# The inverse transform's second stage in 64x64 tiles, in a gated mix of two state-space convolutions

## The chip, the cores and the metric

The kernel runs on one core of a Trainium2 chip. The core has TensorE (PE in the profile; its weight loads are listed apart as PEld), VectorE (DVE), ScalarE (ACT), GpSimd (POOL) and SyncE (SP, which issues every DMA here). The metric is the time of one execution in microseconds on the device; less is better. Before the change it is 507.52 us, the median of three runs (505.0 to 507.69). All data are float32.

## The reference

Two state-space models with their own parameters filter the same signal `u` (2048 steps, 512 channels), and a gate mixes the results. For each channel d, the 128 states n are summed into a kernel K of 2048 taps, and u is convolved with it by FFT. Cut to what matters:

```
g = sigmoid((u * gate_w).sum(-1))                  # one number per time step
# model A (model B is alike, with exp(log_A_real), 2.0 and no B)
K = einsum("dn,dnl,dn->dl", C, exp(dt * A * l), dt * B).real
a = irfft(rfft(u, 2L) * rfft(K, 2L))[:L] + u * Dskip
return g * a + (1 - g) * b
```

## The kernel before, in words

**Tiles.** The 512 channels are cut into eight tiles v of 64 channels, taken in pairs q = v // 2 (four pairs of 128 channels). Each tile holds both models, k = 0 and 1. A time step is l = 64 j + s, with 32 values of j and 64 of s, so a transform of 2048 points is one over j (32 points, the "first stage") and one over s (64 points, 32 different matrices for the indices m, the "second stage").

**A tile's way.** For each of eight chunks of 16 channels (`chunk`) the states' powers are made as tables: POOL multiplies phases and magnitudes (L552, L561, L572, L580: two times 512 elements of `x`, then 512 and 1024 of `E`), ACT takes sine, absolute value and cosine (L592 to L594, 1024 elements each, into the PSUM buffers `sd`), DVE multiplies (L600 to L615), and PE sums over the 128 states (L631, tiles of 128x32) into the bank `kg`. After every second chunk ACT copies the bank to `K` (L653), and `put` does the first stage: 32 matmuls of 64x64 tiles (L674) into two PSUM banks, each copied to `F` by DVE or ACT, as the masks `EV` and `EU` say (L686). When `F` is full, `stage2` takes the 32 indices m in eight groups mg of four: `forward` (L697: four matmuls of 128x128 by 128 columns with `c_g`), the product with the spectrum of u in two DVE operations (L769 and L772: 512 elements each, with the real and the sign-turned imaginary part of u, into `z`), the inverse (L781 and L782: eight matmuls of 128x128 by 128 columns with `c_t`, in pairs that accumulate), a copy by ACT (L785) and a store to HBM (`wt`, L788).

**u.** For each pair, `stage1_u` and `stage2_u` do the same forward transform on u; its spectrum goes to HBM (`ud`, L739) and comes back per tile (L760), 512 KB for two groups mg.

**The end of a pair.** `final` loads `wt` back in another layout (L803) and does the inverse's other stage with weights that contain the gate (L814, 128x64 tiles), in four banks. The loads and sums of a pair come after both its tiles. For the last pair the four loads of a tile go to the buffers in `LAST`.

**The gate.** `gate` sums u * gate_w on PE with a broadcast weight (L843), copies (L852), takes the sigmoid on ACT (L854, 2048 elements), and POOL multiplies it into the weights (L861, L873: 16 operations each of 128x4x32).

**The order.** `Plan` collects operations, each with an engine, a cost, a due time, the buffers that it takes and the operations that it needs. `Plan.run` plays a clock and gives each engine the ready operation that is due first and has its buffers free, and the kernel then issues all of them in that order. So each engine works through a fixed list, and waits where an operand or a buffer is late. The numbers in the tables at the top (`TO`, `LAG`, `FSP` and so on) are due times. SP's list of DMAs is fixed in the same way, and eight semaphores go round: a DMA is issued only once the eighth one before it has landed.

**PSUM.** Eight banks of 128x512: four single ones (`ps`: one for `kg`, two for `forward`, two for `put`, all four for the rest, within the caps), and two double ones (`sd`, 1024 elements) for sine and cosine alone.

## Time and profile before

| What | us |
|---|---|
| median of three runs (505.0 to 507.69) | 507.52 |
| the profiled execution | 506.61 |
| its span, from the first to the last instruction | 504.8 |
| PE busy | 422.9 |
| DVE busy | 398.2 |
| POOL busy | 393.8 |
| ACT busy | 388.8 |

The granted clock of TensorE was 0.949 on average. In the profile's rows, a group of instructions stands as line, engine, operation, out<-in, shape and count, then total busy time in us and mean ns of one, then the engine's idle time before such instructions and who ended it. A row of the timeline is start in us, duration in us, and then the same names. A float32 matmul leaves two records, so counts of matmul records are twice those of the matmuls in the code. A busy time is a union: where instructions of an engine overlap at their ends, that time counts once.

### The profile page before, as it was taken

How to read it: one execution, taken by the hardware profiler on the slowest of the kernel's cores; microseconds unless marked ns; L12 is line 12 of the kernel's file. 1: busy time of each engine (PE TensorE's matmuls, PEld its weight loads, DVE VectorE, ACT ScalarE, POOL GpSimd, SP SyncE). 2: the span in 40 equal slices, each digit the busy share in tenths (PEclk: the TensorE clock that was granted, in tenths of full speed). 3: DMA queues.
4: the chain of work that ended last, by engine and by line, in shares of the span. 5: the costliest groups of instructions: out<-in, count | busy, mean ns of one | idle time of the engine just before them, and what ended most of it. 6: DMA issues, size and time to landing. Idle time of an engine off the chain costs nothing.

```text
span 504.8 us, 21830 instructions
## 1 busy us (share of the span) xinstructions
PE 422.9 (84%) x9584; PEld 383.2 (76%) x9584; DVE 398.2 (79%) x564; ACT 388.8 (77%) x598; POOL 393.8 (78%) x365
## 2 busy tenths in 40 slices
PE   3497996788989999998289986598999899799946
PEld 3397895777767898888279875488989799789936
DVE  5748998989939889999859988978979999863420
ACT  4659989789999887799998778857999878562111
POOL 4674997979969999989898999768979999920000
PEclk9999997699999999999669999789999999989988
DMA  8958773254654455444208676347336157753954
GB/s 284 382 159 270 225 222 122 86 181 117 153 171 130 138 185 149 127 128 128 62 7 248 197 236 214 107 139 219 106 114 195 34 157 229 218 156 115 307 164 189
DMA packets 69438, 85.45 MB, mean 169 GB/s; under 512 B 4704, under 2 KB 50144, under 8 KB 69088
## 3 DMA queue, kind: packets, MB, share of 16 engines
q1 hardware_dynamic: 69344, 84.06, 53.5%
q8 instruction: 75, 1.23, 1.0%
q14 instruction: 19, 0.16, 0.1%
HBM read 50.49 MB, written 33.59 MB: 167 GB/s over the span
## 4 chain that ended last, share of the span: by engine, by line
PE 45%; ACT 20%; DMA 15%; DVE 8%; issue 7%; POOL 3%; SPq 1%; DVEq 0%; ACTq 0%; POOLq 0%
PE ps L697 10%; PE ps L631 8%; PE ps L781 7%; PE ps L782 7%; PE ps L674 6%; PE ps L814 5%; DMA wt<-st 4%; DMA c_g<-in_c_g 3%; DMA X<-wt 3%; ACT sd L592 3%; ACT sd L594 2%; ACT x L593 2%; DMA AB<-in_prm 2%; ACT st L785 2%; DVE z L772 2%
## 5 line engine op out<-in xcount | busy, mean ns | idle before, releaser
L580 POOL TENSOR_TENSOR E<-AB 128x1024 f32<-128x1024 f32 x64 | 125.4, 1960 | 0.1
L781 PE MATMUL ps<-z,c_t 128*128 128x128 f32 x512 | 102.6, 282 | 3.7 <-DVE z L772 1.6
L782 PE MATMUL ps<-z,c_t 128*128 128x128 f32 x512 | 99.9, 277 | 1.2 <-DVE z L772 0.8
L600 DVE TENSOR_TENSOR QD<-sd,E 128x1024 f32<-128x1024 f32 x64 | 77.8, 1216 | 20.3 <-ACT sd L592 9.4
L631 PE MATMUL ps<-E 128*32 128x64 f32 x2048 | 68.1, 230 | 24.5 <-DVE E L610 17.5
L697 PE MATMUL ps<-F,c_g 128*128 128x128 f32 x640 | 85.7, 281 | 3.5 <-ACT F L686 1.3
L781 PEld LDWEIGHTS ps<-z,c_t 128*128 128x128 f32 x512 | 77.6, 191 | 9.0 <-DVE z L772 3.3
L697 PEld LDWEIGHTS ps<-F,c_g 128*128 128x128 f32 x640 | 77.4, 191 | 8.0 <-ACT F L686 1.6
L782 PEld LDWEIGHTS ps<-z,c_t 128*128 128x128 f32 x512 | 77.7, 192 | 2.8 <-DVE z L772 2.7
L631 PEld LDWEIGHTS ps<-E 128*32 128x32 f32 x2048 | 50.9, 115 | 36.5 <-issue 18.9
L561 POOL TENSOR_TENSOR x<-pi,c_tm 128x512 int32<-128x512 int32 x64 | 68.0, 1064 | 13.1 <-ACT sd L594 12.0
L610 DVE TENSOR_TENSOR E<-sd,E 128x1024 f32<-128x1024 f32 x64 | 77.6, 1213 | 0.8 <-ACT sd L594 0.8
L572 POOL TENSOR_TENSOR E<-AB 128x512 f32<-128x512 f32 x64 | 68.5, 1072 | 8.7 <-issue 2.8
L592 ACT ACTIVATE sd<-x 128x1024 f32<-128x1024 int32 x64 | 65.9, 1030 | 9.0 <-DVE QD L605 7.6
L785 ACT COPY st<-ps 128x512 f32<-128x512 f32 x64 | 37.5, 586 | 44.3 <-PE ps L782 25.1
L552 POOL TENSOR_TENSOR x<-gh 128x512 int32<-128x512 int32 x64 | 68.7, 1074 | 0.2
L593 ACT ACTIVATE x<-x 128x1024 f32<-128x1024 int32 x64 | 67.8, 1060 | 1.3
L594 ACT ACTIVATE sd<-x 128x1024 f32<-128x1024 f32 x64 | 66.0, 1032 | 2.6 <-DVE E L615 0.9
L631 PE MATMUL ps<-QD 128*32 128x64 f32 x2048 | 67.1, 228 | 0.1
L769 DVE TENSOR_TENSOR z<-ps,U 128x512 f32<-128x512 f32 x64 | 43.8, 684 | 27.1 <-PE ps L697 23.7
L631 PEld LDWEIGHTS ps<-QD 128*32 128x32 f32 x2048 | 53.0, 116 | 0.0
L674 PE MATMUL ps<-w,K 64*64 64x64 f32 x2048 | 41.0, 230 | 9.0 <-DVE fi L454 3.4
(118 smaller groups left out, 748.9 us busy)
## 6 DMA issues: line engine op xcount, KB each, us to landing
U<-ud SPq DMA_DIRECT2D x32, 512.0 KB, 4.1
wt<-st SPq DMA_DIRECT2D x64, 256.0 KB, 2.7
X<-wt SPq DMA_DIRECT2D x26, 512.0 KB, 5.6
ud<-z SPq DMA_DIRECT2D x32, 256.0 KB, 3.4
U<-in_u SPq DMA_DIRECT2D x16, 256.0 KB, 4.2
ud<-z SPq DMA_DIRECT2D x32, 128.0 KB, 3.4
U<-in_uT SPq DMA_DIRECT2D x16, 256.0 KB, 3.4
out<-st SPq DMA_DIRECT2D x16, 256.0 KB, 5.7
```

Source lines behind the costliest of these rows:

```text
L552: G.tensor_tensor(xi()[:, :, 1, :].rearrange("n c (a b) -> n c a b", a=4), t[:, :, 0:4].unsqueeze(3).to_broadcast([P, NCK, 4, 8]), t[:, :, ...
L580: G.tensor_tensor(Ev()[:, :, 1:3, :].rearrange("n c w t -> n c (w t)"), AA()[:, ca].rearrange("n c w a -> n (c w) a").unsqueeze(3).to_broa ...
L592: op("A", 0.96, e, lambda: A.activation(bv(sn), wv(xi()), AF.Sin, scale=SCL), r=[x], w=[sn], func="S")
L593: op("A", 0.96, e, lambda: A.activation(x.t, x.v(dt=I32), AF.Abs), w=[x])
L594: op("A", 0.96, e, lambda: A.activation(bv(cs), wv(qv(x)), AF.Sin, bias=HALF_PI, scale=-SCL), r=[x], w=[cs], func="S")
L600: lambda: V.tensor_tensor(ev(QD)[:, :, 0::2, :], bv(sn).rearrange("n w c t -> n c w t"), Ev()[:, :, 0::2, :], ALU.mult),
L610: lambda: V.tensor_tensor(Ev()[:, :, 0:2, :], bv(cs)[:, 0].unsqueeze(2).to_broadcast([P, NCK, 2, NJ]), Ev()[:, :, 0:2, :], ALU.mult),
L631: T.matmul(K4[32 * b : 32 * b + 32, gg, :], ev(QD if w else E)[:, c, 2, :], ev(QD if w else E)[:, c, 0:2].rearrange("n h t -> n (h t)"), s ...
L674: T.matmul(bs[h].t[64 * d : 64 * d + 64, 64 * g : 64 * g + 64], K()[64 * h : 64 * h + 64, 64 * g : 64 * g + 64], w1[64 * h : 64 * h + 64, ...
L697: T.matmul(b.v("p (k m h e) -> p m k h e", k=2, m=4, h=32, e=2)[:, mm], Gw[:, m, :], Fv(F)[:, :, m, :].rearrange("p (k h) e -> p k h e", k=2),
L781: T.matmul(o, Tw[:, m, 0:128], zv(Z1), start=True, stop=False)
L782: T.matmul(o, Tw[:, m, 64:192], zv(Z2), start=False, stop=True)
```

## The change

- **The inverse** (`stage2`). The 64 outputs' contraction over 128 rows becomes two of 64 rows each, for the even and the odd points of the spectrum, which stand on the lower and the upper 64 partitions. Per group mg there are 16 matmuls of 64x64 tiles by 128 columns (L867), into the two banks of one `sd` buffer. The matrices `Tx` are half as large as `c_t` was in SBUF, and are gathered from the same input `c_t` by 16 DMAs of 32x32 runs of 128 bytes. `c_g` is loaded into an `F` buffer and four ACT copies put its columns in even and odd order (`Gw`).
- **The product** is one DVE operation of 1024 elements (L852). u's spectrum comes back in four DMAs of 128 KB (L841) in place of one of 512 KB. `stage2_u` writes it once, in 16 DMAs of 512 KB, with one copy of 1024 elements for two groups mg (L810).
- **The gate.** PE sums u * gate_w with u as the weights (L962, 256 matmuls of one column), ACT takes one small exponential, DVE makes the sigmoid of it, PE spreads it over the partitions (L983, 16 matmuls), and DVE makes the weights in four operations of 1024 elements (L992, L995). POOL has no part in it any more. The small weights for this are put together by 17 small DMAs at the start.
- **The end of a pair.** The other stage's matrices are used in tiles of 128x32 (L919, 512 matmuls in place of 256). The loads come in two halves of the banks, 1 MB for each half and tile; for the last tile they are cut in four parts of 256 KB, each behind its own stores. All of them come after the pair's last forward transform (`after=[fwd_last[q]]`). The last tile's staging uses the two `QD` buffers beside the two of `st`.
- **PSUM.** Two single banks (`ps`: `kg` and `forward`, and `final` between them) and three double ones (`sd`) that sine, cosine, first stage, inverse, forward transforms of u, parameters and gate share.
- **Order.** All due times, costs and masks are new. By the masks DVE makes 53 copies of `F` in place of 39, and ACT 43 in place of 57.

The diff, cut to its core (the tables of numbers by a line or two):

```
-EV = (58, 57, 196, 105, 4, 199, 64, 66)
+EV = (66, 186, 8, 94, 210, 141, 62, 216)
-LAST = ("Fp", "AB", "AB", "F")
...
-    "K": (512, 2), "z": (512, 4), "U": (1024, 2),
-    "st": (512, 2), "p": (256, 3), "dtb": (256, 2), "pi": (512, 2), "pf": (256, 2), "al": (512, 1), "fi": (256, 2), "gh": (768, 1), "ps": (512, 4), "sd": (1024, 2),
+    "K": (512, 2), "z": (1024, 2), "U": (1024, 2),
+    "st": (512, 2), "p": (256, 3), "dtb": (256, 1), "pi": (512, 2), "pf": (256, 2), "al": (512, 1), "fi": (256, 2), "gh": (768, 1), "ps": (512, 2), "sd": (1024, 3),
...
-CAPS = {"kg": KG, "kh": KH, "s1": 2, "fb": 4, "pm": 1}
+CAPS = {"kg": KG, "kh": 1, "kl": 2, "fd": FD, "fb": 2, "pm": 1}
...
+    def pair(cls="fd"):
+        b = Buf("sd", cls)
+        return b, [lambda x=x: b.t[:, 512 * x : 512 * x + 512] for x in range(2)]
...
-    Gw, GwB = load("c_g", [P, NJ, P], GWD)
-    Tw, TwB = load("c_t", [P, NJ, 192], TWD)
+    op("D", 0.5, GWD, lambda: DMA(raw_g.v("p (m k) -> p m k", m=NJ, k=P), ins["c_g"]), w=[raw_g], nbytes=4 * P * 4096)
+    for x in range(2):
+        for i in range(2):
+            op(
+                "A", 1.0, GXD,
+                lambda x=x, i=i: A.copy(
+                    Gw[:, 16 * i : 16 * i + 16].rearrange("p m (x r j) -> p m x r j", x=2, r=2)[:, :, x],
+                    raw_g.v("p (m r j x) -> p m r j x", m=NJ, r=2, j=32, x=2)[:, 16 * i : 16 * i + 16, :, :, x],
+                ),
...
+                        DMA(
+                            Tx[o : o + 32, w, :, 32 * d : 32 * d + 32],
+                            ins["c_t"][64 * r + x : 64 * r + 64 : 2, :, 64 * (b + d) : 64 * (b + d) + 32],
+                        )
...
     def put(F, K, items, pos, due, bits):
-        bs = [bank("s1"), bank("s1")]
+        B, bs = pair()
...
     def stage2(v, due, sp):
-            Z1, Z2, hb, st = Buf("z"), Buf("z"), bank(), Buf("st")
+            Z, st = Buf("z"), Buf(("st", "QD")[mg % 2] if v == NV - 1 else "st")
...
-            op("V", 0.6, dm, lambda Z1=Z1, b=b, uv=uv: V.tensor_tensor(m3(Z1.t), m3(b.t), uv(0), ALU.mult), r=[b, U], w=[Z1], hold=[Z2])
-                lambda Z2=Z2, b=b, uv=uv: V.scalar_tensor_tensor(m3(Z2.t), m3(b.t), sgn, uv(1), ALU.mult, ALU.mult),
+                lambda Z=Z, b=b, U=U, y=y: V.tensor_tensor(
+                    Z.t.rearrange("p (w k n) -> p w k n", w=2, k=2),
+                    b.v("p (k n) -> p k n", k=2, n=256).unsqueeze(1).to_broadcast([P, 2, 2, 256]),
+                    U.v("p (w y n) -> p w y n", w=2, y=2, n=256)[:, :, y].unsqueeze(2).to_broadcast([P, 2, 2, 256]), ALU.mult,
+                ),
...
-                for mm in range(4):
-                    T.matmul(o, Tw[:, m, 0:128], zv(Z1), start=True, stop=False)
-                    T.matmul(o, Tw[:, m, 64:192], zv(Z2), start=False, stop=True)
+                for mp in range(2):
+                    for w in range(2):
+                        for o in range(2):
+                            for x in range(2):
+                                p = slice(64 * x, 64 * x + 64)
+                                T.matmul(
+                                    bs[x]()[64 * o : 64 * o + 64, 128 * mp : 128 * mp + 128].rearrange("p (k c) -> p k c", k=2),
+                                    Tx[p, w, 8 * ug + 4 * y + 2 * mp + o, :],
+                                    Z.v("p (w k m c) -> p w k m c", w=2, k=2, m=4, c=64)[p, w, :, 2 * mp + o, :],
+                                    start=(w == 0), stop=(w == 1),
+                                )
...
     def final(q, due):
-                    r=[wt[2 * q + u]], w=[(f, ((u, u + 1),))], nbytes=524288, after=wdone,
+                        r=[(wt[v], ((2 * g0, 2 * g1),))], w=[(f, ((u, u + 1), (g0, g1)))], nbytes=262144 * (g1 - g0),
+                        after=[fwd_last[q]],
...
     def gate(due):
-        op("A", 1.9, d1, lambda: A.activation(gs.t, gs.t, AF.Sigmoid), w=[gs], func="G")
-            op("G", 1.65, d1, weigh, r=[gs, w1iB], w=[(wgB, ((i, i + 1),))])
-            op("G", 1.65, d1, rest, r=[(wgB, ((i, i + 1),)), w1iB], w=[(wgB, ((i + 4, i + 5),))], hold=[wb])
+        op("A", 0.25, d1, lambda: A.activation(gate_[:, 1, :], y.t[:, 0:16], AF.Exp, scale=-1.0), r=[y], w=[gateB], func="E")
+        op("V", 0.4, d1, parts, w=[gateB])
+            op("T", 1.9, d1, wide, r=[gateB, identB], w=[g_])
+            op("V", 1.13, d1, lambda wv=wv, Wv=Wv, gb=gb: V.tensor_tensor(wv(1), gb(), Wv(0), ALU.mult), r=[g_, WB], w=[(wgB, ((2 * i, 2 * i + 1),))])
+                lambda wv=wv, Wv=Wv, gb=gb: V.scalar_tensor_tensor(wv(0), gb(), 1.0, Wv(1), ALU.subtract, ALU.mult),
```

Three places show how instructions move. The first is PE's list in the second stage of the last tile, behind the last first stage. Before, forwards (L697, from the buffer F_67 with c_g) stand in twos and threes, and the inverse of a group (L781, L782, with c_t) is of full-size matmuls in one PSUM bank:

```order
L697 MATMUL ps_101<-F_67,c_g 128x2x64 x4
L697 MATMUL ps_100<-F_67,c_g 128x2x64 x4
L781 MATMUL ps_102<-z_79,c_t 128x128
L782 MATMUL ps_102<-z_80,c_t 128x128
...
L781 MATMUL ps_103<-z_81,c_t 128x128
L782 MATMUL ps_103<-z_82,c_t 128x128
...
L814 MATMUL ps_101<-F_66,X 64x128 x2
L814 MATMUL ps_101<-F_66,wg 64x128 x2
```

With the change, at the same place (L919 is the other stage of the pair before, L774 a forward, L867 an inverse):

```order
L919 MATMUL ps_98<-F_67,wg 32x128 x32
L774 MATMUL ps_99<-F_68,Gw 128x2x64 x4
L774 MATMUL ps_98<-F_68,Gw 128x2x64 x4
L867 MATMUL sd_101<-z_80,Tx 64x128 x16
L774 MATMUL ps_99<-F_68,Gw 128x2x64 x4
L867 MATMUL sd_100<-z_81,Tx 64x128 x16
L774 MATMUL ps_98<-F_68,Gw 128x2x64 x4
L867 MATMUL sd_102<-z_80,Tx 64x128 x16
```

Forwards alternate with inverses, whose 16 matmuls are of 64x64 tiles and write a double buffer `sd`; the other stage of the pair before has moved ahead of this tile's forwards.

The second place is SP's list at the start. Before:

```order
L713 DMA U_83<-in_u 128x512 x2
L713 DMA U_84<-in_u 128x512 x2
L260 DMA gate_w<-in_gate_w 128x4
L301 DMA wp<-in_c_w1i 128x1x64
L260 DMA c_t<-in_c_t 128x6144
L260 DMA c_g<-in_c_g 128x4096
L302 DMA w1i<-wp 128x64
L713 DMA U_83<-in_u 128x512 x2
L713 DMA U_84<-in_u 128x512 x2
L739 DMA ud<-z_80 128x2x256
```

With the change (L340 to L342 and L345 gather the small weights, L307 the matrices Tx):

```order
L790 DMA U_83<-in_u 128x512 x2
L262 DMA gate_w<-in_gate_w 128x4
L286 DMA F_67<-in_c_g 128x4096
L340 DMA wp<-in_c_w1i 16x2x32 x2
L341 DMA wp<-in_c_g 16x2x1
L342 DMA wp<-in_c_g 16x2x1
...
L790 DMA U_82<-in_u 128x512 x2
L307 DMA Tx<-in_c_t 32x32x32 x8
L790 DMA U_83<-in_u 128x512 x2
L345 DMA st_84<-wp 128x66
L307 DMA Tx<-in_c_t 32x32x32 x8
L790 DMA U_82<-in_u 128x512 x2
```

c_g is no longer behind c_t, and 16 small DMAs stand between it and the second pair of loads of u; Tx stands among those loads.

The third place is SP's list at the end. Before, the loads back of the first tile of the last pair (first L803 rows) stand among the stores of the last tile (L788), and those of the last tile behind all stores:

```order
L760 DMA U_83<-ud 128x2x512
L803 DMA F_66<-wt 128x1024
L803 DMA AB_68<-wt 128x1024
L803 DMA AB_69<-wt 128x1024
L803 DMA X<-wt 128x1024
L788 DMA wt<-st_85 128x4x128
...
L788 DMA wt<-st_86 128x4x128
L803 DMA F_66<-wt 128x1024
```

With the change, the loads of the first tile (128 partitions) stand together with the first part of the last tile's (32 partitions), and the other parts come between and behind the last stores (L884):

```order
L884 DMA wt<-st_84 128x4x128
L901 DMA F_66<-wt 128x2x1024
L901 DMA F_66<-wt 32x2x1024
L901 DMA F_67<-wt 128x2x1024
L901 DMA F_67<-wt 32x2x1024
L884 DMA wt<-QD_76 128x4x128
L901 DMA F_66<-wt 32x2x1024
L901 DMA F_67<-wt 32x2x1024
L884 DMA wt<-st_85 128x4x128
L884 DMA wt<-QD_77 128x4x128
```

The first tile's loads have moved behind the last forward transform, nearer to the end, and half of the stores follow them in the queue.

More of the change, by code (lines that the diff above doesn't have):

```diff
@@ L78, in _flat @@
+GD = -10.768
+GSP = 0.866
+GWD = -0.481
+TWD = 8.15
+UAHEAD = -4.959
+UPRE = -3.279
+FPRE = -2.703
+AN = (0.283, -4.034, -2.017, -12.539, -1.507, 3.174, -4.297, 7.068)
+PT = (-7.959, -0.744, 1.469, 2.33)
+PC = (-7.021, -15.911, -16.15, -3.725)
+PO = (-6.761, -2.755, 0.238, -0.262, 0.288, -2.725, 3.118, 0.678)
+AO = (1.468, -0.653, 2.972, -2.371, -4.078)
+CX = 0.854
+CA = 7.157
+CV = 4.779
+CK = -1.063
+CE = 1.619
+CS = -1.44
+FW = -2.905
 def _flat(t):
```

475 lines of the change are left out of this document (267 added, 208 removed).

## The prediction

> **What bounds the kernel now.** I read the page's totals and POOL's slices first, then busy times by stretch, the waits, and the end of the program in order of time.
>
> ```profile
> span 504.8 us, 21830 instructions
> PE 422.9 (84%) x9584; PEld 383.2 (76%) x9584; DVE 398.2 (79%) x564; ACT 388.8 (77%) x598; POOL 393.8 (78%) x365
> POOL 4674997979969999989898999768979999920000
> ```
>
> ```profile
> core 0: us, PE busy (x) PEld busy (x) DVE busy (x) ACT busy (x) POOL busy (x), PEclk, DMA share, GB/s
> 0.00:30.00 30.00, 14.09 (x280) 12.95 (x281) 16.56 (x45) 14.87 (x38) 17.91 (x28) 1.00 0.78 291
> 30.00:60.00 30.00, 26.79 (x816) 24.60 (x815) 25.59 (x36) 27.81 (x46) 20.63 (x17) 1.00 0.81 243
> 60.00:425.00 365.00, 317.34 (x7372) 284.98 (x7373) 321.18 (x440) 317.72 (x475) 335.13 (x306) 0.94 0.49 147
> 425.00:448.00 23.00, 20.31 (x463) 18.58 (x462) 16.79 (x21) 14.02 (x18) 20.14 (x17) 0.93 0.73 225
> 448.00:505.00 57.00, 44.38 (x660) 42.07 (x659) 18.07 (x26) 14.42 (x23) 0.00 (x0) 0.94 0.55 185
> ```
>
> The totals name PE, but the stretches say more. From 60 to 425 us POOL is busy 335.13 of 365 us (92%), DVE 88%, PE and ACT 87%: four engines in one loop of small buffers, none with much room. After 448 us POOL is empty, and 57 us of transforms follow. So I split the span in two: **A**, until POOL's last instruction ends, and **B**, what has to come after it.
>
> ```profile
> ACT st L785 <- PE ps L782: 25.1, 18, 3.6
> DVE z L769 <- PE ps L697: 23.7, 16, 4.2
> POOL AB L506 <- ACT AB L492: 12.7, 6, 4.4
> POOL x L561 <- ACT sd L594: 12.0, 7, 3.5
> ACT st L785 <- DMA wt<-st: 10.9, 4, 8.2
> ACT sd L592 <- DVE QD L605: 7.6, 10, 2.8
> ```
>
> These are waits over the whole span: total us, times, longest. POOL's two largest are for ACT (12.7 + 12.0 = 24.7 us), and the largest waits of ACT and DVE are for PE. PE reaches POOL by way of ACT.
>
> ```profile
> 445.84 1.95 POOL L580 TENSOR_TENSOR E<-AB 128x1024 f32<-128x1024 f32 x1
> 457.06 0.39 PE L641 MATMUL ps<-dskip,c_id 128*128 128x8 f32 x2
> 461.55 1.95 PE L697 MATMUL ps<-F,c_g 128*128 128x128 f32 x16
> 479.05 1.95 PE L697 MATMUL ps<-F,c_g 128*128 128x128 f32 x16
> 492.40 0.70 PE L814 MATMUL ps<-F,X 128*64 128x128 f32 x4 [7.19 <-DMA F<-wt]
> ```
>
> So A is 445.84 + 1.95 = 447.8 us and B is 504.8 - 447.8 = 57.0 us. B has four pieces: 9.3 us to the last table product (457.06), 4.5 us to the first forward transform of the last tile (461.55), 19.4 us to the end of its last forward (479.05 + 1.95 = 481.0), and 23.8 us of last stores, loads back and final transforms.
>
> **The change part by part.** First PE.
>
> ```profile
> 154.57 0.39 PE L782 MATMUL ps<-z,c_t 128*128 128x128 f32 x2
> 157.70 0.39 PE L782 MATMUL ps<-z,c_t 128*128 128x128 f32 x2
> 158.02 0.32 PE L631 MATMUL ps<-E 128*32 128x64 f32 x8
> 161.19 1.16 PE L674 MATMUL ps<-w,K 64*64 64x64 f32 x64
> 162.28 0.32 PE L631 MATMUL ps<-E 128*32 128x64 f32 x8
> ```
>
> From 154.57 to 157.70 fourteen steps of the inverse take 3.13 us, 0.224 us for each full-array matmul of 128 columns; 512 of them are 114.5 us. They become 1024 matmuls of 64x64 tiles by 128 columns. The first stage shows 64x64 tiles by 64 columns: 32 of them (two records each) from 161.19 to 162.28, 34 ns each. With twice the columns the price lies between 34 ns (if issue sets it) and 68 ns (if columns do): 35 to 70 us. I take 56 ns, a quarter of 0.224, as four tiles fill the array: 57 us. The step from 128x128 tiles to 128x32 at 158.02 took 0.32 instead of 0.224 us, 0.10 us more. At most two such steps for each of 64 inverses add 13 us. PE saves 114.5 - 70 = about 45 us, bounds 31 to 80.
>
> The Trainium skill, "TensorEngine Tiling (Array Packing)", section "Tiling Modes" (Key Properties), says that changing the tiling mode drains TensorE, which speaks against alternating forwards and inverses. The row agrees, with 0.10 us. By the rule the saving is 45 us, without it 57; PE is covered by POOL in A either way.
>
> Now the other engines' work.
>
> ```profile
> L600 DVE TENSOR_TENSOR QD<-sd,E 128x1024 f32<-128x1024 f32 x64 | 77.8, 1216 | 20.3 <-ACT sd L592 9.4 <-POOL E L580 4.2 <-PE ps L631 3.5
> L593 ACT ACTIVATE x<-x 128x1024 f32<-128x1024 int32 x64 | 67.8, 1060 | 1.3
> L785 ACT COPY st<-ps 128x512 f32<-128x512 f32 x64 | 37.5, 586 | 44.3 <-PE ps L782 25.1 <-DMA wt<-st 10.9 <-issue 4.2
> L686 DVE COPY F<-ps 128x512 f32<-128x512 f32 x33 | 21.9, 683 | 7.0 <-PE ps L674 7.0
> L873 POOL TENSOR_TENSOR X<-w1i,wg 128x128 f32<-128x128 f32 x16 | 6.8, 467 | 0.0
> L861 POOL TENSOR_TENSOR wg<-X,w1i 128x128 f32<-128x128 f32 x16 | 6.7, 457 | 0.0
> 458.48 0.69 DVE L769 TENSOR_TENSOR z<-ps,U 128x512 f32<-128x512 f32 x1 [3.96 <-PE ps L697]
> 459.09 0.74 DVE L772 SCALAR_TENSOR_TENSOR z<-ps,sgn,U 128x512 f32<-128x512 f32 x1
> 459.75 0.68 DVE L686 COPY F<-ps 128x512 f32<-128x512 f32 x1
> ```
>
> - **POOL** loses the gate's weights: 6.8 + 6.7 = 13.5 us. Nothing is added.
> - **DVE**: a pair of products takes 459.75 - 458.48 = 1.27 us; one of 1024 elements takes about 1.22 (L600), some 0.07 of it under the next one: 1.15. That is 0.12 x 64 = 8 us less. Against it stand four weight operations (4 x 1.22 = 5 us) and, by the new masks, 14 more copies of F (14 x 0.68 = 9.5). The 20 copies of z become 8 twice as wide, some 4 us less. DVE's sum stays within a few us of 398.
> - **ACT** loses those 14 copies of F (about 8 us), the sigmoid and its copies, and gains four copies of c_g (4 x 1.06 = 4.2 us). It ends some 8 us lower.
>
> So only PE and POOL get lighter; DVE and ACT are hardly relieved. In **A**, POOL did 17.9 us before 30 us and 20.63 + 335.13 + 20.14 = 375.9 us in the 418 us behind it, a share of 90%. Of 375.9 - 13.5 = 362.4 us at the same share come 403 us, and A is 433. To that I add relief from PE: I take half of POOL's 24.7 us of waits for ACT away, 12 us, since PE's work falls by about a tenth (45 of 423 us) and some of those waits come from it. The bounds are 0 and all 42 us that POOL idles there. A is 421.
>
> **Startup** can move this.
>
> ```profile
> 8.00 17.61 DMA c_g<-in_c_g
> 25.75 5.46 PE ps L697 x24
> 45.41 1.03 ACT L592 ACTIVATE sd<-x 128x1024 f32<-128x1024 int32 x1
> c_t<-in_c_t SPq DMA_DIRECT2D x1, 3072.0 KB, 13.2
> wt<-st SPq DMA_DIRECT2D x64, 256.0 KB, 2.7
> q1 hardware_dynamic: 69344, 84.06, 53.5%
> ```
>
> Full DMA speed is 291 GB/s / 0.78 = 373 in the first row of the stretches and 225 / 0.73 = 308 in the fourth. Now c_g comes without the 3.1 MB of c_t ahead of it, 8 to 10 us earlier. Then four ACT copies (4.2 us) stand before the first forward (25.75), and 17 small DMAs and 16 of Tx stand in SP's queue among the loads of u, which PE needs in order. I take +1 us on the start of the second chunk's sine (45.41), where POOL's stream begins to flow.
>
> Tx is 16384 runs of 128 bytes, which no row shows. By bytes its 2.1 MB cost 6 to 7 us. By the mean packet, 53.5% x 16 x 504.8 us / 69344 = 62 ns, they cost 16384 x 62 ns / 16 = 63 us. A run of 128 bytes is nearer the bytes' end, since the mean packet has 1.2 KB; and c_t's transfer goes. Both ends are kept for the range.
>
> **B** afterwards: 9.3 and 4.5 us stay. Then eight forwards of 0.98 and six inverses of 0.95 + 0.10 take 14.1 us in place of 19.4, and ACT's longest wait for a store (8.2 us, in this piece) goes, as the last tile has four staging buffers. But the loads back all wait for the last forward: 4.2 MB, with four stores of 1.05 MB among them, take 14 to 17 us, and two landings of some 2 us (a lone store takes 2.7 in all) come on top: 19 us where 492.40 - 481.0 = 11.4 were. The final transforms and stores stay at 504.8 - 492.4 = 12.4. B is 9.3 + 4.5 + 14.1 + 19 + 12.4 = 59.3, 2.3 more than now.
>
> The sum is 421 + 1 + 59.3 = 481 us of span. The profiled execution took 506.61 us, 1.8 more than its span; the median of the three runs is 507.52, 0.9 above it. I forecast **483 us**.
>
> **The rivals.**
> - *Full relief.* If nearly all of POOL's 42 us of idle time comes from PE, A falls to some 30 + 362 + 15 = 407, and the time is 469. For it: the waits for PE above. Against it: DVE would then have to do about 366 us of work (398 less 16.6 in the first 30 us and some 15 in B) in the 386 us up to its last product, 95% where it reaches 88% now.
> - *No relief.* DVE and ACT keep POOL waiting as they do now; only the 13.5 us come. A is 433, the time 433 + 1 + 59.3 + 1.8 = 495. For it: their sums hardly fall. The Trainium skill, "TensorEngine Tiling (Array Packing)", section "Performance Considerations" (PSUM Bottleneck), says that tiling speeds up TensorE but not the emptying of PSUM. The 88% of DVE agree, and this rival is its outcome.
> - *Slower: the shared PSUM buffers.* Sine and cosine had two double banks to themselves; now they share three with every inverse, first stage and parameter step. An inverse holds one for 1.05 us on PE and 0.59 on ACT (L785), a first stage for 1.1 and up to two copies of 0.68, half of one per chunk: about 2.9 us per chunk more, for one buffer more. If half of that shows in ACT's sines, 64 x 1.45 = 93 us, of which ACT's slack (13% of 365 us) hides 47, the time is 483 + 46 = 529. It decides from (507.5 - 483) / 64 = 0.38 us per chunk on. For it: ACT waits in this place already. Against it: 7.6 us in all, 0.12 us per chunk.
> - *The change doesn't get through the startup.* If Tx's runs cost some 25 us beyond c_t, about 40% of the upper bound, PE's loads of u queue behind them and the stream starts some 20 us later: 503.
>
> **How the numbers follow.** Forecast 0.42 (474 to 490), no relief 0.17 (490 to 500), full relief 0.19 (460 to 474), shared buffers 0.14, startup 0.08. The range of 460 to 508 takes in all but the shared buffers and some full relief below 460. A measurement tells about 0.5% here, 2.5 us. Forecast, no relief and full relief are faster, and about half of the startup case: 0.81. The other half is the same, with a slice of the forecast gone wrong: 0.05. Slower: 0.14.
>
> **What would show it.** In the profile after, the inverse should step by about 0.95 us, with 0.1 us before and after it. POOL's busy time should be near 380 us, DVE's near 396, ACT's near 381, PE's below 380. POOL's last instruction should end near 422 us, and 59 us should follow it, with PE waiting some 19 us for the loads from wt. The second chunk's sine should start within a few us of 45. The forecast is wrong if ACT's waits for sd grow above 24 us, if POOL's share between 30 us and its end stays at 90% or below, or if the inverse takes 1.5 us and more.

## The result and the profile after

The changed kernel takes 540.37 us (median of four runs, 535.13 to 540.9) against 507.61 (505.0 to 507.96) for the kernel before: a ratio of 1.0634, 95% interval 1.0559 to 1.0709. It is slower; the forecast was 483. The profiled execution took 540.9 us, 1.8 more than its span. Where some executions of a kernel fell into a slower state of the chip, the ratio leaves them out and the median in us does not, so that e18's 513.51 us and 1.0115 below do not follow from one another by division.

First the totals of the page after, POOL's slices, and its queue of instruction loads (packets, MB, share).

```profile
span 539.1 us, 25870 instructions
PE 389.1 (72%) x11632; PEld 347.2 (64%) x11632; DVE 397.1 (74%) x510; ACT 384.4 (71%) x580; POOL 380.2 (71%) x331
...
POOL 4733799736896799776989996958989999900000
...
q8 instruction: 91, 1.49, 1.2%
```

All four sums of work fell or stayed, DVE, ACT and POOL within 4 us of the forecast; PE saves 34 us in place of 45. The span grew by 34 us all the same. So the time did not go into work as these sums count it, it went into waits. Busy times by stretch, as before:

```profile
0.00:30.00 30.00, 12.25 (x377) 11.47 (x381) 17.64 (x47) 19.39 (x41) 19.20 (x27) 1.00 0.60 177
30.00:60.00 30.00, 21.57 (x563) 20.51 (x556) 18.06 (x27) 19.33 (x33) 8.59 (x7) 1.00 0.71 180
60.00:425.00 365.00, 275.60 (x8391) 244.36 (x8389) 300.45 (x373) 294.90 (x440) 306.75 (x263) 0.89 0.45 138
...
471.20:539.10 67.90, 42.27 (x1099) 37.96 (x1098) 17.78 (x18) 14.57 (x23) 0.00 (x0) 0.81 0.53 149
```

Three places differ. Between 30 and 60 us POOL works 8.59 us where it worked 20.63. From 60 to 425 us it is busy 84% in place of 92%, while **every** engine is less busy than before (PE 275.60 in place of 317.34) and the granted clock is 0.89 in place of 0.94. And 67.9 us follow POOL's last instruction in place of 57.0. The waits over the whole span:

```profile
POOL x L621 <- ACT sd L654: 33.1, 13, 12.1
DVE F L744 <- PE sd L732: 31.4, 14, 7.1
...
POOL E L632 <- PE ps L689: 26.5, 11, 5.2
...
PE ps L689 <- issue: 14.9, 13, 3.1
...
PE sd L732 <- DMA U<-in_u: 14.0, 3, 7.4
...
DVE F L744 <- ACT F L744: 11.8, 6, 4.9
...
PE sd L732 <- issue: 11.3, 7, 2.9
...
ACT sd L652 <- DVE QD L665: 10.8, 12, 4.2
...
POOL AB L558 <- ACT AB L544: 3.3, 3, 1.6
```

POOL's waits for ACT at its phases (L561 before, L621 after) went from 12.0 to 33.1 us, while those at `AB` fell from 12.7 to 3.3; its waits for PE's table products went from 2.6 to 26.5. New is that PE itself waits for nothing that the profile shows ("issue"): 14.9 + 11.3, and 5.2 more at the gate's matmuls, 31 us. The kernel before has hardly any:

```profile
POOL E L572 <- PE ps L631: 2.6, 1, 2.6
...
PE ps L674 <- issue: 1.8, 2, 1.3
...
PE ps L631 <- issue: 0.9, 2, 0.7
```

PE's timeline of the changed kernel shows one such pause:

```profile
213.79 0.32 PE L689 MATMUL ps<-QD 128*32 128x64 f32 x8
215.77 0.44 PE L689 MATMUL ps<-E 128*32 128x64 f32 x8 [1.66 <-issue]
215.94 0.49 PE L689 MATMUL ps<-QD 128*32 128x64 f32 x8
```

It falls into the middle of a group of table products whose operands are all there, and behind it, at half clock, eight records take 0.21 us in place of 0.11. What comes in between is the end of a block of instructions. The q8 row has 91 packets for the changed kernel's 11632 matmul records and as many weight loads, so a block holds about 128 of each. In the records of that queue no two blocks start closer than 3.32 us (before: 3.36), 26 ns per matmul record. Table products go through theirs at 17 ns (8 records in 0.11 us), the first stage too. And the pauses between 88 and 150 us stand 83, 82, 81, 78, 77, 76, 76, 75 and 75 records behind a multiple of 128, so they return once per block. All 26 pauses of this kind in the profile end 2.2 to 3.1 us after a packet of that queue started, and so do the 23 of the changed kernel's second profile. That PE waits there for its next block is therefore read off the trace. Why it happens in this kernel and hardly in the one before is another question. The inverse before used 112 ns per record (16 in 1.79 us), now it uses 32 ns (32 records in 1.03 us), so the long inverses may have given the next block time to come in; e1 below speaks against that.

That gives two theories. **Supply:** PE runs dry of instructions where short matmuls stand together, and the loop, in which POOL, ACT, DVE and PE wait for each other in fixed lists, loses what PE loses. **Buffers:** the shared double PSUM buffers hold the loop, as the rival in the prediction had it, and PE is only the last to be named. A third, **work**, says that PE's matmul time still counts. Startup and end are apart.

### The profile page after: what moved, and what is told of

Same layout as the page of the kernel before. It is cut to its first block, busy times and chain, and to the rows that moved or that the text cites. A ratio compares the mean times of both kernels' runs of the same rounds, so it can differ in the third digit from the quotient of the medians.

```text
span 539.1 us, 25870 instructions
## 1 busy us (share of the span) xinstructions
PE 389.1 (72%) x11632; PEld 347.2 (64%) x11632; DVE 397.1 (74%) x510; ACT 384.4 (71%) x580; POOL 380.2 (71%) x331
## 3 DMA queue, kind: packets, MB, share of 16 engines
q8 instruction: 91, 1.49, 1.2%
## 4 chain that ended last, share of the span: by engine, by line
PE 39%; DVE 19%; ACT 14%; issue 13%; DMA 10%; SPq 3%; POOL 1%; DVEq 0%; ACTq 0%
PE sd L732 8%; PE ps L689 8%; PE ps L774 7%; PE sd L867 7%; DVE z L852 4%; PE ps L919 3%; DVE E L670 3%; ACT sd L652 3%; PE sd L759 3%; DVE QD L660 3%; DMA F<-wt 3%; DMA F<-in_c_g 2%; DVE QD L665 2%; ACT x L653 2%; DVE E L675 2%
## 5 line engine op out<-in xcount | busy, mean ns | idle before, releaser
L852 DVE TENSOR_TENSOR z<-ps,U 128x1024 f32<-128x1024 f32 x64 | 77.8, 1220 | 27.4 <-PE ps L774 23.9
L621 POOL TENSOR_TENSOR x<-pi,c_tm 128x512 int32<-128x512 int32 x64 | 67.8, 1060 | 35.6 <-ACT sd L654 33.1
L867 PE MATMUL sd<-z,Tx 64*64 64x128 f32 x2048 | 73.4, 283 | 22.4 <-DVE z L852 14.6
L632 POOL TENSOR_TENSOR E<-AB 128x512 f32<-128x512 f32 x64 | 68.4, 1070 | 28.7 <-PE ps L689 26.5
L689 PE MATMUL ps<-E 128*32 128x64 f32 x2048 | 75.0, 239 | 17.9 <-issue 9.3
L774 PE MATMUL ps<-F,Gw 128*128 128x128 f32 x512 | 80.2, 304 | 8.9 <-DVE z L852 6.6
L774 PEld LDWEIGHTS ps<-F,Gw 128*128 128x128 f32 x512 | 69.0, 208 | 18.4 <-DVE z L852 8.4
L867 PEld LDWEIGHTS sd<-z,Tx 64*64 64x64 f32 x2048 | 58.2, 137 | 31.8 <-DVE z L852 6.8
L652 ACT ACTIVATE sd<-x 128x1024 f32<-128x1024 int32 x64 | 65.8, 1028 | 15.2 <-DVE QD L665 10.8
L732 PE MATMUL sd<-w,K 64*64 64x64 f32 x2048 | 45.2, 246 | 31.9 <-ACT K L711 14.4
L744 DVE COPY F<-sd 128x512 f32<-128x512 f32 x53 | 34.9, 686 | 43.3 <-PE sd L732 31.4
L732 PEld LDWEIGHTS sd<-w,K 64*64 64x64 f32 x2048 | 40.2, 157 | 36.6 <-ACT K L711 15.6
L877 ACT COPY st<-sd 128x512 f32<-128x512 f32 x60 | 35.0, 584 | 24.9 <-PE sd L867 24.5
```

The costliest lines, as they stand in the source:

```text
L632: G.tensor_tensor(Ev()[:, :, 0, :].rearrange("n c (a b) -> n c a b", a=4), A1()[:, ca, ::-1].unsqueeze(3).to_broadcast([P, NCK, 4, 8]), BB ...
L652: op("A", 1.01, e, lambda: A.activation(bv(sn), wv(xi()), AF.Sin, scale=SCL), r=[x], w=[sn], func="S")
L689: T.matmul(K4[32 * b : 32 * b + 32, gg, :], ev(QD if w else E)[:, c, 2, :], ev(QD if w else E)[:, c, 0:2].rearrange("n h t -> n (h t)"), s ...
L732: T.matmul(bs[h]()[64 * d : 64 * d + 64, 64 * g : 64 * g + 64], K()[64 * h : 64 * h + 64, 64 * g : 64 * g + 64], w1[64 * h : 64 * h + 64, ...
L774: T.matmul(b.v("p (k m h e) -> p m k h e", k=2, m=4, h=32, e=2)[:, mm], Gw[:, m, :], Fv(F)[:, :, m, :].rearrange("p (k h) e -> p k h e", k=2),
L852: lambda Z=Z, b=b, U=U, y=y: V.tensor_tensor(Z.t.rearrange("p (w k n) -> p w k n", w=2, k=2), b.v("p (k n) -> p k n", k=2, n=256).unsqueez ...
```

## The experiments

Ratios are to the kernel before, run beside each experiment on the same chip. The changed kernel was run again beside e9, e10 and e11, and is the measure there. The other runs are compared with it by their ratios (1.0579 and 1.0634), whose intervals are about 1% wide on each side, so gains and losses of 5 us or less are not clear of noise.

> The changed kernel itself, as the measure for the runs of this call: 535 to 541 us, ratio 1.056 to 1.071.

535.28 us, ratio 1.0579 (1.0482 to 1.0677), as expected.

### Startup

```
-                        DMA(
-                            Tx[o : o + 32, w, :, 32 * d : 32 * d + 32], ...
+                DMA(Tx[o : o + 32], ins["c_tx"][o : o + 32])
...
+        DMA(wp_t.rearrange("m x o d c -> (m x o d) c"), ins["c_wl"])
```

> The changed kernel in the same order, with Tx laid out ready in a constant and loaded in 4 DMAs in place of 16 (16 KB runs instead of 128 bytes), and the last weights in one DMA in place of 16. Theory (the loads of u queue behind these DMAs on SP's queue and in the DMA engines): the third load of u is no longer waited for, POOL's pause of 12.1 us at 32 us falls below 3 us, and the time falls by 10 to 13 us, to 528 to 531. Rival (startup loss comes from elsewhere, from the four copies of c_g or the order): within 4 us of 540.

530.46 us, ratio 1.048 (1.0404 to 1.0556): 1.0 to 1.5% less than the changed kernel, 5 to 8 us, less than expected, and clear of its first measurement but not of its second (1.0482 to 1.0677). SP's timeline of the changed kernel shows how the loads of u stand among the others:

```profile
24.83 7.43 SPq L307 DMA_DIRECT2D Tx<-in_c_t  x8
32.36 0.98 SPq L790 DMA_DIRECT2D U<-in_u  x2
33.40 0.42 SPq L345 DMA_DIRECT2D st<-wp  x1
33.87 7.77 SPq L307 DMA_DIRECT2D Tx<-in_c_t  x8
41.74 1.42 SPq L790 DMA_DIRECT2D U<-in_u  x2
```

Sixteen DMAs of Tx hold SP's queue for 15.2 us, 0.95 each. The loads of u between and behind them land 3.6 to 3.9 us after their issue, as the median of all such loads does (3.9): they were issued late, not moved slowly. PE waits for U, and ACT's copy of u's transform (L810) waits 8.20 us for PE with a cosine behind it in ACT's list, for which POOL waits 12.1. With the mended loads that wait of POOL is 4.82 us and the waits of PE for these loads fall from 14.0 to 0.2:

```profile
36.80 1.06 POOL L608 TENSOR_TENSOR x<-pi,c_tm 128x512 int32<-128x512 int32 x1 [4.82 <-ACT sd L641]
```

```profile
PE sd L719 <- DMA U<-in_u: 0.2, 1, 0.2
```

By 60 us POOL has worked 36.25 us (27.79 in the changed kernel, 38.55 before). So the startup theory holds, and the startup is a quarter of the loss at most. The edit makes the DMAs fewer and their runs longer at once, so it does not say which of the two held the queue.

### Less or more PE work, fewer records

```
 e1:  T.matmul(bs[o]()[...], Tx[:, w, two m, :], Z[:, w, ...])      # 8 of the full array for 16 tiles
 e6:  for w in range(1)                                             # 8 of 16 tile matmuls
 e10: products(): for w in range(1)                                 # 16 of 32 table matmuls
 e9:  if q and (b, a) != (1, 3): continue                           # most of the gate's sums left out
 e4:  T.matmul(y.t[:, j : j + 1], t.t[:, 128 * ba : 128 * ba + 128], gw[:, q : q + 1], ...)
```

> The changed kernel, in the same order of instructions, with each inverse done by 8 matmuls of the full array (128x128 weights, 128 columns) in place of 16 in 64x64 tiles. It leaves out the split: both halves are summed, so the values are another computation with the same shapes and dependences. PE gets about 44 us more matmul time (1.79 in place of 1.10 us for each of 64 inverses) and 1024 records of matmuls and as many weight loads less. Theory A (PE runs dry of instructions, loses its full clock in the pauses, and that holds the loop): 520 to 532 us, PE's waits put down to issue halved from 33 us, half clock below 90 us. Theory B (the shared double PSUM buffers hold the loop): each inverse holds one 0.7 us longer, 545 to 560 us. Theory C (PE's matmul time counts): 550 us or more.

556.98 us, 1.1049 (1.0977 to 1.112): slower by 21 to 24 us than the changed kernel. Theory A failed here, and its sign too: the waits for issue hardly fell, though the inverses are as long again as in the kernel before and 1024 records are gone:

```profile
PE ps L689 <- issue: 12.0, 11, 1.9
...
PE sd L732 <- issue: 11.0, 8, 4.1
...
PE sd L960 <- issue: 2.9, 2, 2.0
```

With 0.4 us more at L917 that is 26 us, where the changed kernel has 33 and 29 in its two profiles, counting all places, and the kernel before 3. So the shorter inverse is not why PE runs dry, and in this order of instructions it is worth 21 to 24 us, by its work on PE or by its shorter hold of a buffer. What makes the difference of 26 to 3 us is not shown; the order and the final transforms in narrower tiles differ as well, and the gate's sums, but e9 below leaves most of those out and keeps 29 us of such waits.

> The changed kernel in the same order; the second of the two products of each inverse is left out (8 matmuls in 64x64 tiles in place of 16). PE gets 35 us less work and 1024 records less. Theory A (supply of instructions): 518 to 530 us, near the kernel with the full array, which has as few records but 79 us more PE work. Theory C (PE's matmul time): 515 us, and at least 25 us below the full array. Theory B: the buffers are held 0.55 us shorter per inverse, 525 to 535 us.

531.24 us, 1.051 (1.0439 to 1.058): about 5 us less. Both runs have 1024 records less. Between them lie 26 us of time, and 61 us of PE's busy time in their profiles (428.1 and 367.4; 79 us at full clock by the expectation). So some two fifths of PE's busy time counts, or the time for which an inverse holds its double PSUM buffer does: both runs came out in the ranges that Theory B gave (545 to 560, 525 to 535), and they change the work and the hold together. The inverse's records alone do not count: at 32 ns each they cost about what their loading costs. Supply in the form of the expectation (every record counts) falls.

> The changed kernel in the same order, with the gate's sums done by 128 matmuls whose weights are 128 columns of u in place of 512 with 32 columns each (u's columns laid out for it; the same result). 384 records of matmuls and as many weight loads less, all in the stretch from 126 to 160 us. Theory A' (PE's supply of instructions, one block of 128 matmuls each 3.3 us or more, holds the loop only where many short matmuls stand together: first products, table products and these): PE's waits put down to issue fall by 6 us or more, the long stretch of half clock from 137 to 164 us is broken up, and the time falls by 6 to 12 us against the changed kernel, a ratio to the kernel before of 1.040 to 1.052. Theory A'' (the supply does not hold the loop, as the run with 1024 records less in the inverses suggests): ratio 1.058 to 1.068.

545.71 us, 1.0807 (1.0711 to 1.0903): slower than either theory gave. The counts of matmuls in this expectation and in the next are those of records; the matmuls are about half of that (here 64 for 256). The wide ones cost PE more than the pauses that they save: 16 records take 3.57 us at half clock.

```profile
146.05 3.57 PE L958 MATMUL sd<-gate_w,U 128*128 128x1 f32 x16
```

> The changed kernel in the same order; of the 512 matmuls of the gate's sums only 152 are left (all for the first quarter of u, one column for the others), so the gate is not the reference's. 360 records of matmuls and weight loads less between 126 and 160 us, and nothing in their place. Theory A' (PE holds the loop in that stretch, by its supply of instructions and by half clock): the time falls by 8 us or more against the changed kernel in this call, and the half clock from 137 to 164 us shrinks. Rival (POOL's pauses there come from the order, the parameter steps and the shared buffers): it falls by less than 4 us.

537.92 us, 1.0622 (1.0537 to 1.0706): no gain over the changed kernel beside it (1.0579). The run left 88 of 256 matmuls of the gate's sums, 336 records less. The gate's sums on PE are not the cause.

> The changed kernel in the same order with the second of the two table products of each chunk left out (16 of 32 matmuls), so the tables are not the reference's: 2048 records of matmuls and as many weight loads less, some 35 us of PE's time at full clock, in the dense places. Theory A' (PE's time and its supply of instructions hold the loop): 20 us or more below the changed kernel, ratio 1.025 or less, waits for issue below 15 us. Rival (order and buffers hold it, PE is only named last): less than 10 us.

520.47 us, 1.0279 (1.0183 to 1.0375): 15 us less than the changed kernel, between the two theories.

```
-                for w in range(2):
+                for w in range(1):      # the same edit in the kernel before
```

> The kernel before with the same half of the table products left out, as the measure for the run above. Theory A' for the changed kernel says nothing of this one; by its own waits (PE 84% busy, 3.4 us of waits for issue) I expect 3 to 8 us less, ratio 0.984 to 0.994. If it falls as far as the changed kernel does, the table products hold both alike, and the difference of the two kernels lies elsewhere.

498.24 us, 0.9807 (0.9697 to 0.9917): 9 us less. The table products hold both kernels, the changed one more by these medians, though 15 and 9 us are not clear of each other; work and supply are not yet apart.

### Records at the same PE time

This run is to tell them apart: 32 short records of 17 ns are replaced by 4 long ones.

```
-                for w in range(2):
+                for w in range(1):
...
+            for h in range(2):
+                T.matmul(kg.t[:, ko + 128 * h : ko + 128 * h + 128], ident, QD.t[:, 0:128], start=False, stop=False)
```

> The changed kernel in the same order with the second of the two table products of each chunk (16 matmuls in 128x32 tiles, 32 records, about 0.5 us) replaced by 2 matmuls of the full array with 128 columns (4 records, about 0.45 us), so the tables are not the reference's. PE's time per chunk stays within 0.1 us; 1792 records of matmuls and as many weight loads less. Theory A (PE waits for its instructions, which come in blocks of 128 matmuls of which the next is ordered only in the middle of the one at work): the time falls nearly as far as with the products left out, to a ratio of 1.015 to 1.035, waits for issue halved. Rival (PE's time at work): no gain, ratio 1.05 to 1.07.

517.66 us, 1.0248 (1.0162 to 1.0334): 17 to 19 us less than the changed kernel, at 385.2 us of PE's busy time (383.1 in the changed kernel's second profile). The clock was not what it gained by: 0.875 in its profile, 0.893 and 0.899 in the two of the changed kernel. PE's waits put down to issue are 12 us in place of 31:

```profile
PE sd L735 <- issue: 7.3, 9, 2.0
...
PE sd L965 <- issue: 2.7, 1, 2.7
...
PE ps L689 <- issue: 1.9, 2, 1.3
```

> The same replacement in the kernel before (1792 records of matmuls less at the same PE time). Theory A: a gain here too, but smaller, since its inverses, 16 records in 1.79 us, gave the next block time to come: ratio 0.975 to 0.992. Rival: ratio 0.997 to 1.01.

502.29 us, 0.9951 (0.9916 to 0.9986): 2.5 us less, which lies between the two ranges expected. The same replacement is worth 3.3 to 3.9% to the changed kernel and 0.5% to the one before. So the replacement takes away some 15 of the 30 us between the two kernels, and less work of PE is not the reason: a chunk's products take 1.30 us with the replacement and 1.10 without (medians of the traces). That the waits for instruction blocks are the reason fits the fall of PE's waits for issue. One rival is not excluded: the long matmuls read `QD` and not `E`, so PE is done with `E` 0.65 us after a chunk's first product in place of 0.99, and POOL may write the next `E` sooner. In the changed kernel POOL waited for that 11 times; 11 x 0.34 = 4 us is my estimate of it at that place. e10 frees `E` as early and gains no more, and e17 cannot tell, since the kernel before hardly waits there (2.6 us).

```
-                    T.matmul(o, Tw[:, m, 0:128], zv(Z1), start=True, stop=False)
+                    for k in range(2):
+                        T.matmul(o[:, k], Tw[:, m, 0:128], zv(Z1)[:, k], start=True, stop=False)
```

> The kernel before, with each matmul of the inverse cut into two of half the columns (64 in place of 128): the same result, PE's matmul time nearly the same, 1024 records of matmuls and as many weight loads more, spread evenly over the 64 inverses. Theory A (every record counts): ratio 1.02 or more, with PE's waits for issue up from 3 us to 15 us or more. Theory A' (only dense places count): ratio 0.995 to 1.012.

599.56 us, 1.1873 (1.1775 to 1.1971), but not for the reason expected: the waits for issue stay at 3.9 us. PE's busy time rose by 108.5 us, from 422.9 to 531.4, for 512 more matmuls: 0.21 us for one of 64 columns, where one of 128 took 0.224. The run says nothing on supply; it shows that a matmul of the full array with 64 columns has nearly the price of one with 128.

```profile
span 600.8 us, 23878 instructions
...
PE 531.4 (88%) x10608; PEld 495.5 (82%) x10608; DVE 397.9 (66%) x564; ACT 391.4 (65%) x598; POOL 395.0 (66%) x365
```

### The shared buffers

```
 e3:  for q, b in pcs: b.t = raw[q].t[:, 2560:3584]                 # after the order is made
 e7:  def evict(h=h, e=V.tensor_copy if (nsplit[0] if split else bits >> h) & 1 else A.copy):
```

> The changed kernel in the same order, with the buffer of the second parameter step (held about 11 us, four times) put into free space of the parameters' own SBUF tile, so that this step holds none of the three shared double PSUM buffers. Theory B (holds of the shared buffers): the waits of PE and ACT for the end of this step go (PE L759 for DVE L495: 3.0 us at 110 us, and the half clock behind it), 525 to 535 us. Theory A (instruction supply and clock): within 5 us of 540.

549.85 us, 1.09 (1.0841 to 1.0959): slower, and it does not decide. DVE's products of the step, which took 0.43 us with one operand in PSUM, take up to 1.4 us on average with both in SBUF, and DVE's sum rises by 13.6 us:

```profile
L476 DVE TENSOR_TENSOR AB<-AB 128x256 f32<-128x256 f32 x4 | 5.6, 1411 | 0.0
...
L496 DVE TENSOR_TENSOR AB<-AB,pf 128x256 f32<-128x256 f32 x4 | 4.9, 1225 | 0.1
```

```profile
L493 DVE TENSOR_TENSOR sd<-sd,pf 128x256 f32<-128x256 f32 x4 | 1.7, 432 | 0.1
...
L473 DVE TENSOR_TENSOR sd<-AB,sd 128x256 f32<-128x256 f32 x4 | 1.7, 428 | 0.1
```

> The changed kernel in the same order, but where the two copies of a first stage's pair were split between VectorE and ScalarE (some 20 pairs), both go to one engine, in turns. In the changed kernel such copies never run side by side: the second waits for the first, 20.5 us of waits (DVE F for ACT F 11.8, ACT F for DVE F 8.7), which the kernel before did not have, since its halves lay in two buffers. Theory D (these ordered copies hold the loop): the time falls by 5 to 12 us, ratio 1.040 to 1.053. Rival (the waits fall in slack): ratio 1.058 to 1.068; it may also rise, as a copy that stood beside another now stands behind it.

540.91 us, 1.0711 (1.0616 to 1.0805): no gain. That two copies out of one double buffer wait for each other is true of the profile and costs nothing that this edit gives back. The price of the sharing as a whole could not be tried: all eight banks are in use. So the buffers stay open as a cause: of their direct tests e3 was spoiled and e7 reached the copies alone, and e1 and e6 fit them.

### Together, and in another order

e8 joins the edits of e2, e4 and e7; e18 those of e2 and e14. In e15 and e16 `order = pl.run()` becomes `order = [pl.ops[i] for i in ORDER]`.

> The changed kernel in the same order with three things mended together: Tx and the last weights in few large DMAs, the gate by 128 wide matmuls, the split pairs on one engine. If the three add up (8 to 10 us of startup, 6 to 12 of the gate, 5 to 12 of the pairs): ratio 1.00 to 1.025. If POOL's waits only move to the next engine: ratio 1.035 to 1.048, as with the startup alone.

542.51 us, 1.0753 (1.0666 to 1.0841). Against the changed kernel the startup gave -1.0 to -1.5%, the wide gate cost 1.7 to 2.3%, the copies 0.8 to 1.3%; their sum, 1.0 to 2.6%, takes in what the three cost together, 1.2 to 1.7%. It was the expectation that had two of the signs wrong.

> The changed kernel in its own order with the startup mended and with the second table product of each chunk replaced by two long matmuls of the same PE time (so the tables are not the reference's). If the two effects are separate they add: 1.2% of the startup and 3.5% of the instructions, ratio 1.008 to 1.022. If they are the same time twice: ratio 1.022 to 1.035.

513.51 us, 1.0115 (1.0064 to 1.0166), the sum of the two, as expected. So the startup and the table products' records are separate losses, and 1.6% (8 us) stay between this run and e17, the kernel before with the same tables.

> The changed kernel with the startup mended (Tx and last weights in few DMAs) and with another order of the same operations on each engine: the work, the buffers and the result are unchanged. The order was found by moving operations one at a time in a list that counts PE's waits for its blocks of instructions and the half clock behind a stretch in which PE is less than half busy. Theory A (the two bite because of what stands next to what): 25 us or more below the mended startup alone, ratio 0.98 to 1.015, waits for issue and half clock both down by a third. Rival (the split itself costs the time, in any order): within 8 us of it, ratio 1.035 to 1.055.

522.36 us, 1.0333 (1.0264 to 1.0402): 8 us less than e2, far less than Theory A gave and at the edge of the rival's range. The waits for issue did not fall, while the mean clock rose from 0.880 in e2's profile to 0.904:

```profile
PE sd L785 <- issue: 15.8, 13, 2.3
...
PE ps L742 <- issue: 11.5, 9, 4.0
...
PE sd L1015 <- issue: 4.1, 3, 1.9
```

> The kernel before, its operations put in another order by the same procedure, as the measure for the run above. Theory A: a gain here too, but a smaller one in PE's waits for issue, as it has only 3 us of them: ratio 0.95 to 0.98. If it does not gain and the changed kernel does, the split was only badly ordered; if both gain alike, the split stays behind in the best order found.

497.04 us, 0.983 (0.9774 to 0.9885), faster than both kernels, with the kernel before's work and result. Both kernels gain about 8 us by a new order (1.5 and 1.7%), and the changed kernel stays behind in the best order that was found. So its loss isn't one of its first order alone, as far as these two orders tell.

## Why the prediction was wrong, point by point

- **The work.** Right: POOL 380.2 us (near 380 forecast), DVE 397.1 (396), ACT 384.4 (381). The inverse takes 1.03 to 1.10 us at full clock in place of 0.95, which is 64 to 69 ns per matmul, at the upper bound of 68 and not at the 56 taken; a forward beside it takes 1.09 in place of 0.98, the 0.10 us of the changed tiling. PE ended at 389.1, not below 380: more of its work ran at half clock.
- **"PE is covered by POOL in A either way"**, "Of 375.9 - 13.5 = 362.4 us at the same share come 403 us" and "I take half of POOL's 24.7 us of waits for ACT away". This is the step that failed. The sum let POOL keep its share of busy time and raised it further, to 93% of the time from 30 us to its end; the share fell from 90% to 82%, and POOL's last instruction ends at 471.2 us in place of 421:

```profile
469.21 1.97 POOL L640 TENSOR_TENSOR E<-AB 128x1024 f32<-128x1024 f32 x1
```

  The 24.7 us of waits for ACT did not halve, they are 36.4 (33.1 + 3.3), and those for PE's table products went from 2.6 to 26.5. The sum had no term for a PE that waits for its instructions, and 1 us for the startup. e14 puts the table products' records at 17 to 19 us (some of it perhaps `E`); by the profiles 8 to 13 of them lie ahead of POOL's end (458.6 us, against 471.2 and 467.0 in the changed kernel), the rest behind it. e2 puts the startup at 5 to 8 us. Together that is 13 to 21 of the 50 us that A missed. The other 29 to 37 us stay open. They are about the size of the gain that had been counted on, 15 us for POOL's lost work and 12 for its waits. The saving on PE did not fail by itself: e1, with the long inverse in the same order, is 21 to 24 us slower. What failed is that nothing else in the change would slow POOL.
- **Startup.** The term was +1 us. By 60 us POOL had lost 10.8. The prediction weighed Tx's bytes and its runs of 128 bytes; what the trace shows is SP's queue held for 0.95 us by each of 16 DMAs, with loads of u behind them. The startup rival had the mechanism, loads of u that queue behind Tx, but put it at 20 us.
- **B.** 59.3 forecast, 67.9 measured. The wait for the loads was 16.5 us (19 forecast). The pieces before and after it were longer: 18.3 us to the last tile's first forward in place of 13.8, 18.8 for its forwards and inverses in place of 14.1, and the final transforms ran at half clock at first, behind the wait, 14.4 in place of 12.4. A part is PE's pauses again (1.30 and 0.82 us). Its rows:

```profile
483.31 0.82 issue
484.13 2.40 PE sd L732 x77
...
501.86 9.54 DMA F<-wt
...
511.43 0.03 issue
511.46 8.60 DMA wt<-st
```

  These are not the whole of the 8 us left between e18 and e17. In one profiled execution of each (516.33 and 501.05 us) the time behind POOL's last instruction is 61.8 and 56.7 us, 5 us apart, and POOL's last instruction ends at 452.8 and 442.6, 10 us apart. No run took the end alone.
- **The rivals.** The slower one had the right sign; its mechanism is neither shown nor excluded. ACT's waits for `sd` behind DVE's `QD`, the row that the prediction read, are 10.8 us (7.6 before); with all other waits of ACT for `sd` they are 23.0 (10.3 before), just short of the 24 named as a sign, and 0.20 us more per chunk where the rival needed 0.38. e7 gave nothing, e3 did not decide. The Trainium skill's rule on the emptying of PSUM ("TensorEngine Tiling (Array Packing)", section "Performance Considerations"), which stood behind "no relief", did not decide either: DVE and ACT are less busy than before. No case stood for PE's supply, though the profile before had what it takes: 75 blocks in its q8 row, none closer than 3.36 us to the next, and table products at 17 ns per record. So the range ended at 508.

## What to carry to other kernels

Where many short matmuls stand together, compare their records with the blocks that the profile's instruction queue brings in that time, and look for "issue" in the waits of PE. An engine whose work is taken away does not hand that time to the others where all work through fixed lists: a forecast that keeps the share of the busiest engine needs a term for each new wait that the change can bring, here for instructions, for loads of u and for shared buffers. And a load cut into many small DMAs can be paid in the queue that issues them, by whatever stands behind it there.

## What the runs showed of the hardware

**In these profiles half clock follows a stretch in which PE is about half busy or less.** The clock's records change only every 3.41 us. Five such stretches of the changed kernel (length, PE, PEld, DVE, ACT, POOL busy, then the granted clock):

```profile
208.93:212.34 3.41, 2.46 (x98) 2.15 (x98) 3.28 (x6) 2.06 (x4) 3.41 (x4) 1.00 1.00 407
212.34:215.75 3.41, 1.18 (x36) 0.86 (x36) 3.41 (x5) 2.73 (x5) 3.33 (x5) 1.00 0.99 356
215.75:219.16 3.41, 3.39 (x66) 2.93 (x65) 3.24 (x9) 1.54 (x2) 3.41 (x6) 0.50 0.77 229
219.16:222.58 3.42, 1.29 (x68) 1.02 (x64) 0.25 (x2) 2.25 (x6) 3.00 (x3) 1.00 0.32 87
222.58:225.99 3.41, 3.01 (x14) 3.02 (x15) 3.27 (x5) 3.38 (x4) 0.65 (x1) 0.50 0.72 217
```

PE is busy 1.18 of 3.41 us, with the pause of 1.66 us in it: the next stretch has half clock. There it is busy 3.39, and the one after has the full clock again. Over both kernels' profiles, 23 of the 24 stretches behind which the clock fell had PE busy for half or less (one had 0.62), and all behind which it rose 0.87 or more; full clock was kept from 0.47 up. So a pause of PE can be paid twice. The mean clock was 0.893 after and 0.949 before. The Trainium skill, "TensorE: Matmul & The Clock Gate", Part 1, gives the length of such a window as 3.4 us, which agrees, and speaks of an idle window; here a half-idle one sufficed.

**PE's instructions come in blocks of 256.** The changed kernel's 11632 matmuls and 11632 weight loads came in 91 packets, the 9584 of each of the kernel before in 75, e1's 10608 in 83 and e14's 9840 in 77, just under 256 to the packet each time. In no profile here do two blocks start closer than 3.22 us (e2; 3.32 in the changed kernel's first profile). The Trainium skill, "Runtime: NRT & Kernel Launch", section "Instruction fetch mechanics", states the block of 16 KiB and calls the crossing mostly hidden. The block agrees (1.49 MB in 91 packets); here it is not hidden (31 us of pauses), and the measurement decides.

**A product of two SBUF operands on DVE waits for the instruction that POOL is at.** In e3's trace, of the eight products at L476 and L496 two ran beside an idle POOL and took 0.42 us. The other six started while POOL was in an operation, ended 0.28 us after that operation's end, and took 1.17 to 2.17 us. With one operand in PSUM such a product took 0.43 us in the changed kernel all the time.
